# Six full dummy products at the top, and block 0's second half decoded in round 4 ahead of the Prelu

## The chip, the cores and the metric

The kernel runs on one core of a Trainium2 chip. The metric is the device time of one launch in microseconds (us), the median of three runs. Five things run side by side on the core: TensorE (PE, with its weight loads shown apart as PEld), VectorE (DVE), ScalarE (ACT), GpSimd (POOL), and DMA transfers that SyncE (SP) issues.

## The reference

A chunked linear-attention scan over 4 batches, 8 heads and 768 steps (32 channels and 16 states a head) is followed by a two-layer network on its 3072 tokens of width 256. Cut to what matters:

```
for each chunk c:
    M       = (C_c B_c^T) * L_c                      # L: decays inside the chunk, causal
    y_c     = M x_c + (C_c state) * decay_to_i
    state   = decay_full * state + B_c^T (x_c * decay_from_j)
h   = y @ w_in          # [3072, 256] @ [256, 2048]
g   = max(0.01 * h, h)
out = g @ w_out         # [3072, 2048] @ [2048, 256]
```

The weights come as 64-bit floats and are turned into 32-bit floats on the chip.

## The kernel before, in words

The steps are worked on in 12 chunks of 64. The hidden width is cut in 16 blocks `f` of 128, the tokens in 6 tiles `t` of 512. The order of the work on each engine is the order in which the program is written; each engine works its own list in that order, and an instruction that has to wait holds up all that stand behind it on its engine.

**Start.** While the first inputs arrive, PE runs dummy products of zeros on the tile `idle` (128x512, `keep_warm`, line 276) and then 38 tiny ones of 32x32 (line 303). `sum_rows` (line 380), the first product of use, stands behind them. It needs the logarithms of `la`.

**Rounds.** The loop at line 683 runs rounds `c` = 2 to 12. A round makes, in PE's order: `scores` of chunk c (line 465), the first layer of block `f = c - 3` for tile 0 (`ffn_in`, line 192), `outputs` of chunk c-1 (lines 553 and 565), `states` (line 483), a decay product for chunk c+2 (`decays`, line 522), the second layer of the block before (`ffn_out`, line 161), and the other decay product. DVE multiplies the scores with the decays (`weigh`, line 473), decodes weights, makes the low part `gl` of the hidden values (line 199) and keeps the states (`keep_state`, line 495). ACT makes exponentials, the copies `cm` of C (`spread_c`, line 456), the two Prelus of `ffn_in` (lines 196 and 197), and copies of the outputs (line 575).

**Decoding a weight block.** A block's 64-bit words land in `raw` (line 101), 256 KB in a half. `dec_abs` (ACT, line 112), `dec_clamp`, `dec_shift`, `dec_sign`, `dec_low` (DVE, lines 116, 122, 129, 136) turn them into 32-bit floats in `w32`. `dec_high` (ACT, line 142) copies these into the high part `wha`, and `dec_rest` (line 145, POOL or DVE) writes what is left into the low part `wla`. Each product of the network is made three times, high by high, low by high, high by low. Block 0's columns for the first layer (IN) and for the second (OUT) are decoded apart. `ffn_out` of block 0, at the end of round 4, is the first to need the OUT half.

**After the scan** the remaining blocks are decoded in a loop over (f, t) steps up to some 150 us, and tiles 2 to 5 are worked on by a seven-product scheme for 2x2 matrices, in which PE is nearly never idle.

Of the kernel before, what the change touches and what calls it, by code (L numbers as in the profile page):

```python
# [36 lines left out]
DIRECT = 2  # L37
STACKED = (3, 4)
SLOTS = 5
WARM = 3  # L40
SHORT = 38
AHEAD = 4
FIRST = 3
NEARLY = NC - FIRST + 1
# [8 lines left out]
def scan_ffn(ctx: ExitStack, tc: tile.TileContext, a_l, bcn_l, x_l, w_l, out_l):  # L53
    nc = tc.nc
    PSUM = bass.MemoryType.PSUM
    dve, act, pool, pe, sp = nc.vector, nc.scalar, nc.gpsimd, nc.tensor, nc.sync
# [31 lines left out]
    def weight(half, f):  # L88
        return wa[half][:, f] if f < NFA else wb[half][:, f - NFA]
# [13 lines left out]
    def w32(f):  # L103
        if f not in w32s:
            w32s[f // 2 * 2] = w32_pool.tile([128, 2, 2 * DM], F32, name="w32")
            w32s[f // 2 * 2 + 1] = w32s[f // 2 * 2]
        return w32s[f][:, f % 2]

    ALL, IN, OUT = slice(None), slice(0, DM), slice(DM, 2 * DM)

    def dec_abs(f, c=ALL):
        act.activation(w32(f)[:, c], raws[f][:, c, 1].bitcast(F32), AF.Abs)

    def dec_clamp(f, c=ALL):
        w = w32(f)[:, c]
        dve.tensor_scalar(
            out=w, in0=w, scalar1=MAG_MIN, scalar2=MAG_MAX, op0=ALU.max, op1=ALU.min,
        )

    def dec_shift(f, c=ALL):  # L120
        w = w32(f)[:, c].bitcast(U32)
        dve.tensor_scalar(
            out=w, in0=w, scalar1=3, scalar2=0x3FFFFFFF,
            op0=ALU.logical_shift_left, op1=ALU.bitwise_and,
        )

    def dec_sign(f, c=ALL):
        w = w32(f)[:, c].bitcast(U32)
        dve.scalar_tensor_tensor(  # L129
            out=w, in0=raws[f][:, c, 1], scalar=0xC0000000, in1=w,  # L130
            op0=ALU.bitwise_and, op1=ALU.bitwise_or,
        )

    def dec_low(f, c=ALL):
        w = w32(f)[:, c].bitcast(U32)
        dve.scalar_tensor_tensor(
            out=w, in0=raws[f][:, c, 0], scalar=29, in1=w,
            op0=ALU.logical_shift_right, op1=ALU.bitwise_or,
        )

    def dec_high(f, c=ALL):
        act.copy(weight(0, f)[:, c], w32(f)[:, c])  # L142

    def dec_rest(f, eng=None, c=ALL):
        (eng or dve).tensor_tensor(  # L145
            out=weight(1, f)[:, c], in0=w32(f)[:, c], in1=weight(0, f)[:, c], op=ALU.subtract
        )
# [56 lines left out]
    pa, pb = (psum.tile([128, 2, TS], F32, name=n) for n in ("pa", "pb"))  # L204
# [24 lines left out]
    idle = cst.tile([128, TS], BF16, name="idle")  # L229
# [44 lines left out]
    def keep_warm(n, space):  # L274
        for _ in range(n):
            pe.matmul(
                space, lhsT=idle[:, :128], rhs=idle[:, :space.shape[-1]], start=True, stop=True
            )
# [20 lines left out]
        dve.memset(blk[64 * hp:64 * hp + 64, hp], 1.0)  # L299
    dve.memset(later, 0.0)  # L300
    keep_warm(WARM, pa[:, 0])
    for _ in range(SHORT):
        pe.matmul(pa[:32, 0, :32], lhsT=idle[:, :32], rhs=idle[:, :32], start=True, stop=True)
    pool.affine_select(
        out=sign, in_=sign, pattern=[[-3, 2 + GB]], compare_op=ALU.is_ge, fill=0.0, base=-ROW,
        channel_multiplier=1,
# [151 lines left out]
    def scores(c):  # L458
        for b in range(NB):
            bp, st = divmod(b, 2)  # L460
            o = (st * NH2 + bp) * Q
            cols = slice(o, o + Q)
            for g in range(NG):
                r = slice(32 * g, 32 * g + 32)
                pe.matmul(  # L465
                    sspace[g // 2][64 * st:64 * st + 64, g % 2, bp].rearrange(
                        "p (h i) -> p h i", h=2),
                    lhsT=bs[c][r, cols], rhs=cms[c][r, :, cols], start=True, stop=True,
                )

    def weigh(c, half):
        m = lts[c].rearrange("p (a g h) i -> p a g (h i)", a=NH2, g=NG)[:, :, 2 * half:2 * half + 2]
        dve.tensor_tensor(
            out=m, in0=sspace[half].rearrange("p g a x -> p a g x"), in1=m, op=ALU.mult,
        )

    def states(c):
        for b in range(NB):
            bp, st = divmod(b, 2)
            r = slice(64 * st, 64 * st + 64)  # L480
            for g in range(NG):
                u = (bp * NG + g) * 2
                pe.matmul(  # L483
                    zspace(c)[32 * g:32 * g + 32, st * NH2 + bp],
                    lhsT=bnd[c][r, u:u + 2].rearrange("p h n -> p (h n)"),
                    rhs=xs[c][r, u:u + 2].rearrange("p h d -> p (h d)"),
                    start=True, stop=True, skip_group_check=True,
                )
# [38 lines left out]
    def passed(c):  # L527
        for st in range(2):
            pe.matmul(
                espace[:, st * NH2:(st + 1) * NH2], lhsT=esel,  # L530
                rhs=er[:, (c - STACKED[0]) * 2:(c - STACKED[0]) * 2 + 2, st * Q:(st + 1) * Q],
                start=True, stop=True, skip_group_check=True,
            )

    def passed_exp(c):
        es[c] = p3.tile([128, CT], F32, name="es")
        act.activation(
            by_part(es[c]), espace.rearrange("p (s b) i -> p s b i", s=2), AF.Exp
        )
# [45 lines left out]
    def split_out(o, low):  # L585
        hi, lo, v = (v[:, :, o * CT:(o + 1) * CT] for v in (xh[1], xl[1], xf1))
        if low:
            pool.tensor_tensor(out=lo, in0=v, in1=hi, op=ALU.subtract)
        else:
            pool.tensor_copy(hi, v)  # L590
# [85 lines left out]
    def next_decay(c, h):  # L676
        if c < NC:
            if h == 0:
                alloc_lt(c)
            decays(c, h)  # L680
            decay_exp(c, h)

    for c in range(2, NC + 1):
        f = c - FIRST
        if c < NC:
            scores(c)
        if c < AHEAD:
            states(c - 1)
        if c + 1 in STACKED:
            passed(c + 1)  # L690
            passed_exp(c + 1)
        if c == 2:
            for h in range(2):
                next_decay(3, h)
            dec_abs(0, IN)
        if c < NC:
            weigh(c, 1)
            weigh(c, 0)
        if c < AHEAD:
            keep_state(c - 1)  # L700
        if c == 3:
            dec_abs(1)
        if c + 1 < NC:
            spread_c(c + 1)
            weigh_c(c + 1)
        if c < NC - 1:
            weigh_b(c)
        if 6 <= c < 10:
            split_out(*divmod(c - 6, 2))
        if f >= 0:  # L710
            low = ffn_in(f, 0, HB[0])
        else:
            fill_slots(3, 4, dve.tensor_copy)
            dec_clamp(0, IN)
            dec_shift(0, IN)
            send_rows(5, 7)
            send_cols(5, NC, sp)
            fetch_bc(4, "t")
            fetch_w(2, (0,))
            fetch_exp(5)  # L720
            fetch_bc(5, "bc")
            fetch_w(2, (1,))

        if c == 4:
            dec_high(0, OUT)
            dec_rest(0, pool, OUT)
        if c > 2:
            for g in (dec_clamp, dec_shift, dec_sign, dec_low):
                g(f + 1)
        if c > 3:  # L730
            fetch_bc(c + 2, "b")
        if c > 2:
            fetch_w(c, (0,))
        if c > 3:
            fetch_bc(c + 2, "c")
        outputs(c - 1)
        if AHEAD <= c < NC:
            states(c - 1)
        keep_out(c - 1)
        if f >= 0:  # L740
            low()
        if c == 3:
            dec_abs(0, OUT)
            for g in (dec_clamp, dec_shift, dec_sign, dec_low):
                g(0, OUT)
        if AHEAD <= c < NC:
            keep_state(c - 1)
        if c == 2:
            end_decay(c)
            low_out(1)  # L750
        if c > 2:
            fetch_w(c, (1,))
        if c > 3:
            fetch_exp(c + 2)
        if c > 2:
            fetch_bc(c + 2, "t")
            fetch_x(c + 1)
        if c in (4, 7):
            send_rows(*{4: (7, 10), 7: (10, 12)}[c])
        next_decay(c + 2, 0)  # L760
        if c > 2:
            decode_high(f + 1)
            if c < NC - 1:
                end_decay(c)
            if f + 2 <= NFA:
                dec_abs(f + 2)
        if len(queue) > 1:
            ffn_out(*queue.popleft())
        else:
            keep_warm(2, HB[0] if c == 2 else o01[:, 1])  # L770
        if c == 2:
            decays(4, 1)
            dec_sign(0, IN)
            dec_low(0, IN)
            dec_high(0, IN)
            dec_rest(0, pool, IN)
            decay_exp(4, 1)
        else:
            next_decay(c + 2, 1)
# [247 lines left out]
```

## Time and profile before

| | |
|---|---|
| median of 3 runs | 324.14 us (318.23, 324.14, 324.59) |
| profiled execution | 323.78 us |
| its span on the core | 322.1 us |
| PE busy | 307.0 us (95%), 3049 instructions |
| PE weight loads | 238.8 us, 3049 instructions |
| DVE / ACT / POOL busy | 216.9 / 188.1 / 83.4 us |

The sum below is made against the profiled execution. A row of the timeline gives start, duration, engine, line and operation, and in brackets how long the engine had been idle before it and what ended that. The chain of waits follows the work that ended last back to its start; its rows give start, length, engine and line.

### The profile page before, as it was taken

How to read it: one execution, taken by the hardware profiler on the slowest of the kernel's cores; microseconds unless marked ns; L12 is line 12 of the kernel's file. 1: busy time of each engine (PE TensorE's matmuls, PEld its weight loads, DVE VectorE, ACT ScalarE, POOL GpSimd, SP SyncE). 2: the span in 40 equal slices, each digit the busy share in tenths (PEclk: the TensorE clock that was granted, in tenths of full speed). 3: DMA queues.
4: the chain of work that ended last, by engine and by line, in shares of the span. 5: the costliest groups of instructions: out<-in, count | busy, mean ns of one | idle time of the engine just before them, and what ended most of it. 6: DMA issues, size and time to landing. Idle time of an engine off the chain costs nothing.

```text
span 322.1 us, 7449 instructions
## 1 busy us (share of the span) xinstructions
PE 307.0 (95%) x3049; PEld 238.8 (74%) x3049; DVE 216.9 (67%) x354; ACT 188.1 (58%) x353; POOL 83.4 (26%) x115
## 2 busy tenths in 40 slices
PE   8987799997999999999999999999999999999994
PEld 4444477665688887887878888888888888888883
DVE  6589478886789498853776566676576555665551
ACT  7675767774375567654764467644576436554451
POOL 6245347564267345951000100000000000000000
PEclk9999899998999999999999999999999999999999
DMA  6576976664124000000020000000003000000003
GB/s 184 145 239 169 293 247 188 201 186 160 58 78 133 1 0 0 2 0 0 26 107 0 0 1 3 0 0 2 0 18 113 2 0 0 2 1 0 1 2 130
DMA packets 17926, 21.67 MB, mean 67 GB/s; under 512 B 3300, under 2 KB 10724, under 8 KB 17892
## 3 DMA queue, kind: packets, MB, share of 16 engines
q1 hardware_dynamic: 17732, 21.16, 21.1%
q8 instruction: 24, 0.39, 0.5%
q14 instruction: 10, 0.08, 0.1%
q10 hardware_dynamic: 160, 0.04, 0.1%
HBM read 17.80 MB, written 3.39 MB: 66 GB/s over the span
## 4 chain that ended last, share of the span: by engine, by line
PE 78%; DVE 8%; ACT 5%; issue 4%; POOL 1%; DMA 1%; SPq 0%; DVEq 0%; ACTq 0%; POOLq 0%
PE o L161 35%; PE h L161 22%; PE h L192 8%; PE pa L465 2%; PE pa L553 1%; DVE w L129 1%; DMA raw<-w_l 1%; PE pa L565 1%; DVE wlb L145 1%; ACT h L197 1%; DVE gl L199 1%; PE pd L522 1%; PE pb L483 1%; PE pb L565 1%; ACT gh L196 1%
## 5 line engine op out<-in xcount | busy, mean ns | idle before, releaser
L935 ACT ACTIVATE gh<-tmp 128x512 fp32r<-128x512 f32 x48 | 30.2, 629 | 49.7 <-DVE tmp L959 46.4
L161 PE MATMUL o<-gh,wha 128*128 128x512 f32 x132 | 53.2, 403 | 1.2 <-ACT wha L142 1.2
L161 PE MATMUL o<-gl,wha 128*128 128x512 f32 x132 | 52.2, 396 | 0.5 <-DVE gl L199 0.5
L161 PE MATMUL o<-gh,wla 128*128 128x512 f32 x132 | 52.2, 396 | 0.3 <-POOL wla L145 0.3
L937 DVE TENSOR_TENSOR gl<-tmp,gh 128x512 fp32r<-128x512 f32 x48 | 33.2, 692 | 22.2 <-ACT tmp L936 22.2
L199 DVE TENSOR_TENSOR gl<-h,gh 128x512 fp32r<-128x512 f32 x32 | 21.8, 684 | 14.4 <-ACT h L197 14.4
L196 ACT ACTIVATE gh<-h 128x512 fp32r<-128x512 f32 x32 | 19.1, 597 | 21.1 <-PE h L192 21.1
L936 ACT ACTIVATE tmp<-tmp 128x512 f32<-128x512 f32 x48 | 30.3, 632 | 1.5
L161 PEld LDWEIGHTS o<-gh,wha 128*128 128x128 f32 x132 | 25.0, 189 | 6.6 <-ACT wha L142 1.5
L161 PEld LDWEIGHTS o<-gl,wha 128*128 128x128 f32 x132 | 25.2, 191 | 6.3 <-DVE gl L199 1.0
L161 PEld LDWEIGHTS o<-gh,wla 128*128 128x128 f32 x132 | 24.9, 189 | 5.7 <-POOL wla L145 0.6
L161 PE MATMUL h<-oph,wsh 128*128 128x512 f32 x64 | 25.0, 391 | 0.0
L161 PE MATMUL h<-oph,wsl 128*128 128x512 f32 x64 | 24.9, 389 | 0.0
L161 PE MATMUL h<-opl,wsh 128*128 128x512 f32 x64 | 24.9, 389 | 0.0
L954 DVE TENSOR_TENSOR tmp<-h,tmp 128x512 f32<-128x512 f32 x16 | 11.1, 691 | 19.9 <-PE h L161 19.9
L145 POOL TENSOR_TENSOR wla<-w,wha 128x512 fp32r<-128x512 f32 (+1 forms) x12 | 14.3, 1193 | 35.3 <-ACT wha L142 32.8
L161 PE MATMUL o<-gh,whb 128*128 128x512 f32 x60 | 23.3, 389 | 0.0
L161 PE MATMUL o<-gh,wlb 128*128 128x512 f32 x60 | 23.3, 389 | 0.0
L161 PE MATMUL o<-gl,whb 128*128 128x512 f32 x60 | 23.3, 389 | 0.0
L952 ACT COPY tmp<-h 128x512 f32<-128x512 f32 x16 | 9.4, 590 | 20.8 <-PE h L161 20.8
L197 ACT ACTIVATE h<-h 128x512 f32<-128x512 f32 x32 | 19.0, 595 | 0.0
L192 PE MATMUL h<-xh,wha 128*128 128x512 f32 x44 | 18.5, 420 | 0.0
(176 smaller groups left out, 695.7 us busy)
## 6 DMA issues: line engine op xcount, KB each, us to landing
raw<-w_l SPq DMA_DIRECT2D x32, 256.0 KB
xs<-x_l SPq DMA_DIRECT2D x12, 256.0 KB
out_l<-ob SPq DMA_DIRECT2D x9, 256.0 KB
bs<-bcn_l SPq DMA_DIRECT2D x12, 128.0 KB
cs<-bcn_l SPq DMA_DIRECT2D x12, 128.0 KB
ts<-bcn_l SPq DMA_DIRECT2D x12, 128.0 KB
es<-esums SPq DMA_DIRECT2D x18, 64.0 KB
out_l<-wtmp SPq DMA_DIRECT2D x3, 256.0 KB
```

Source lines behind the costliest of these rows:

```text
L145: (eng or dve).tensor_tensor(out=weight(1, f)[:, c], in0=w32(f)[:, c], in1=weight(0, f)[:, c], op=ALU.subtract)
L161: pe.matmul(space, lhsT=w, rhs=x, start=start and i == 0, stop=stop and i == 2, skip_group_check=again,)
L192: pe.matmul(hp, lhsT=w[k][low_w], rhs=(xh, xl)[low_x][t][:, k], start=i == 0, stop=i == 5,)
L196: act.activation(gh, hp, AF.Prelu, alpha=0.01)
L197: act.activation(hp, hp, AF.Prelu, alpha=0.01)
L199: return lambda: dve.tensor_tensor(out=gl, in0=hp, in1=gh, op=ALU.subtract)
L465: pe.matmul(sspace[g // 2][64 * st:64 * st + 64, g % 2, bp].rearrange("p (h i) -> p h i", h=2), lhsT=bs[c][r, cols], rhs=cms[c][r, :, cols ...
L935: act.activation(gh, v, AF.Prelu, alpha=0.01)
L936: act.activation(v, v, AF.Prelu, alpha=0.01)
L937: return g, lambda: dve.tensor_tensor(out=gl, in0=v, in1=gh, op=ALU.subtract)
L952: act.copy(a, A)
L954: dve.tensor_tensor(out=u2, in0=B, in1=a, op=ALU.add)
```

## The change

`WARM` goes from 3 to 6 and the 38 tiny products are gone. In round 3, `dec_sign` and `dec_low` of block 0's OUT half no longer stand at the end of the round. They stand in round 4 behind the two `weigh` of that round, with `dec_high` and `dec_rest` of that half right behind them, ahead of `ffn_in`; and `dec_rest` is on DVE where it was on POOL.

```
-WARM = 3
-SHORT = 38
+WARM = 6
...
     keep_warm(WARM, pa[:, 0])
-    for _ in range(SHORT):
-        pe.matmul(pa[:32, 0, :32], lhsT=idle[:, :32], rhs=idle[:, :32], start=True, stop=True)
...
         if 6 <= c < 10:
             split_out(*divmod(c - 6, 2))
+        if c == 4:
+            dec_sign(0, OUT)
+            dec_low(0, OUT)
+            dec_high(0, OUT)
+            dec_rest(0, dve, OUT)
         if f >= 0:
             low = ffn_in(f, 0, HB[0])
...
-        if c == 4:
-            dec_high(0, OUT)
-            dec_rest(0, pool, OUT)
         if c > 2:
             for g in (dec_clamp, dec_shift, dec_sign, dec_low):
                 g(f + 1)
...
         if c == 3:
             dec_abs(0, OUT)
-            for g in (dec_clamp, dec_shift, dec_sign, dec_low):
-                g(0, OUT)
+            dec_clamp(0, OUT)
+            dec_shift(0, OUT)
```

DVE from the end of round 3 to the end of round 4, before (`w32_461` with 256 columns is block 0's OUT half, `w32_689` block 2, `lt_547` the decays of chunk 4, `ss_807` the states that chunk 4's outputs read):

```order
L199 TENSOR_TENSOR gl0_61<-h0_89,gh0_60 128x512
L116 TENSOR_SCALAR w32_461<-w32_461 128x256
L122 TENSOR_SCALAR w32_461<-w32_461 128x256
L129 SCALAR_TENSOR_TENSOR w32_461<-raw_393,w32_461 128x256
L136 SCALAR_TENSOR_TENSOR w32_461<-raw_393,w32_461 128x256
L473 TENSOR_TENSOR lt_547<-pb_95,lt_547 128x2x256
L473 TENSOR_TENSOR lt_547<-pa_94,lt_547 128x2x256
L116 TENSOR_SCALAR w32_689<-w32_689 128x512
L122 TENSOR_SCALAR w32_689<-w32_689 128x512
L129 SCALAR_TENSOR_TENSOR w32_689<-raw_483,w32_689 128x512
L136 SCALAR_TENSOR_TENSOR w32_689<-raw_483,w32_689 128x512
L199 TENSOR_TENSOR gl1_63<-h0_89,gh1_62 128x512
```

The same stretch of DVE in the changed kernel, whose line numbers are one lower at the top and three lower from line 304 on (`w32_426` is block 0, `w32_652` block 2, `lt_512` chunk 4's decays):

```order
L115 TENSOR_SCALAR w32_426<-w32_426 128x256
L121 TENSOR_SCALAR w32_426<-w32_426 128x256
L470 TENSOR_TENSOR lt_512<-pb_95,lt_512 128x2x256
L470 TENSOR_TENSOR lt_512<-pa_94,lt_512 128x2x256
L128 SCALAR_TENSOR_TENSOR w32_426<-raw_358,w32_426 128x256
L135 SCALAR_TENSOR_TENSOR w32_426<-raw_358,w32_426 128x256
L144 TENSOR_TENSOR wla_59<-w32_426,wha_58 128x256
L115 TENSOR_SCALAR w32_652<-w32_652 128x512
L121 TENSOR_SCALAR w32_652<-w32_652 128x512
L128 SCALAR_TENSOR_TENSOR w32_652<-raw_448,w32_652 128x512
L135 SCALAR_TENSOR_TENSOR w32_652<-raw_448,w32_652 128x512
L198 TENSOR_TENSOR gl1_63<-h0_89,gh1_62 128x512
```

The two multiplications come two instructions earlier; the sign, the low bits and the new `wla` stand between them and block 2's decoding.

ACT in round 4, before (`raw_483` is block 2, `lt_682` chunk 5's decays, `gh1` and `h0` the Prelus of block 1):

```order
L112 ACTIVATE w32_689<-raw_483 128x512
L449 ACTIVATE lt_682<-pd_96 128x512
L456 ACTIVATE cm_713<-cs_490,odd_131 128x256 x2
L196 ACTIVATE gh1_62<-h0_89 128x512
L197 ACTIVATE h0_89<-h0_89 128x512
L142 CAST wha_58<-w32_461 128x256
L575 COPY xf1_126<-pa_94 128x256
```

and in the changed kernel:

```order
L111 ACTIVATE w32_652<-raw_448 128x512
L446 ACTIVATE lt_645<-pd_96 128x512
L453 ACTIVATE cm_676<-cs_455,odd_131 128x256 x2
L141 CAST wha_58<-w32_426 128x256
L195 ACTIVATE gh1_62<-h0_89 128x512
L196 ACTIVATE h0_89<-h0_89 128x512
L572 COPY xf1_126<-pa_94 128x256
```

The copy of block 0's OUT half has passed the two Prelus; it still stands behind block 2's `dec_abs`.

## Rows read from the trace of the kernel before

**Rows 1.** The page, its fourth part: the chain's shares of the span by engine.
```profile
PE 78%; DVE 8%; ACT 5%; issue 4%; POOL 1%; DMA 1%; SPq 0%; DVEq 0%; ACTq 0%; POOLq 0%
```

**Rows 2.** The chain of waits in order of time: start us, us, what.
```profile
1.26 1.46 PE pa L276 x3
2.72 1.12 PE pa L303 x38
...
28.98 3.88 DMA raw<-w_l
...
34.03 0.80 ACT cm L456 x2
...
36.19 0.74 POOL wla L145
36.98 1.91 PE o L161 x5
...
39.33 0.41 PE pa L465 x2
40.42 1.93 PE h L192 x6
...
98.63 0.60 DVE wlb L145
```

**Rows 3.** Timeline of PE, 1 to 14 us.
```profile
6.92 1.91 PE L373 MATMUL pd<-lt,after 128*128 128x512 f32 x2
...
11.73 1.12 PE L373 MATMUL pd<-lt,after 128*128 128x512 f32 x2
```

**Rows 4.** Timeline of ACT, round 4.
```profile
35.72 0.39 ACT L142 CAST wha<-w 128x256 fp32r<-128x256 f32 x1
```

**Rows 5.** Timeline of DVE, end of round 3 and round 4.
```profile
29.42 1.38 DVE L129 SCALAR_TENSOR_TENSOR w<-raw,w 128x256 uint32<-128x256 uint32 x1
...
33.58 0.43 DVE L116 TENSOR_SCALAR w<-w 128x512 f32<-128x512 f32 x1 [0.82 <-ACT w L112]
...
35.23 0.69 DVE L136 SCALAR_TENSOR_TENSOR w<-raw,w 128x512 uint32<-128x512 uint32 x1
...
36.76 0.61 DVE L495 SCALAR_TENSOR_TENSOR ss<-pb,odd,tmp 128x128 f32<-128x128 f32 x2 [0.24 <-ACT xf L575]
```

**Rows 6.** Timeline of POOL at the same time.
```profile
29.19 1.33 POOL L145 TENSOR_TENSOR wla<-w,wha 128x512 fp32r<-128x512 f32 x1 [3.14 <-ACT wha L142]
```

**Rows 7.** The chain of waits at the start of round 10.
```profile
71.64 0.53 DVE ss L495 x2
...
72.21 0.33 PE pb L465 x2
```

**Rows 8.** Stretches: busy us (count) of PE, PEld, DVE, ACT, POOL; granted clock; DMA share; GB/s.
```profile
37.00:42.00 5.00, 5.00 (x44) 3.23 (x44) 1.85 (x5) 2.63 (x6) 3.17 (x4) 0.66 0.85 218
78.00:83.00 5.00, 4.94 (x63) 3.34 (x63) 1.28 (x4) 1.48 (x3) 1.86 (x2) 0.66 0.30 103
```

**Rows 9.** Timeline of PE: the two waits in `states` that no engine ended.
```profile
57.09 0.33 PE L483 MATMUL pb<-xs,bnd 64*32 64x64 f32 x10 [1.04 <-issue]
...
78.06 0.42 PE L483 MATMUL pb<-xs,bnd 64*32 64x64 f32 x21 [2.02 <-issue]
```

**Rows 10.** The page, its third part: queue, kind: packets, MB, share of 16 engines.
```profile
q8 instruction: 24, 0.39, 0.5%
```

**Rows 11.** The same view of 54.4 to 55.6 us alone.
```profile
q8 instruction: 1, 0.02, 5.2%
```

**Rows 12.** Stretches, columns as in rows 8: counts of PE's instructions between places.
```profile
57.05:78.05 21.00, 18.52 (x511) 13.29 (x512) 17.15 (x29) 14.44 (x30) 12.12 (x14) 1.00 0.59 179
52.43:55.83 3.40, 3.40 (x152) 2.62 (x134) 2.87 (x5) 2.40 (x6) 3.40 (x5) 1.00 0.82 271
39.79:43.73 3.94, 3.94 (x147) 2.95 (x136) 3.10 (x6) 2.30 (x6) 1.31 (x2) 0.83 0.83 235
59.47:62.86 3.39, 3.39 (x144) 2.60 (x137) 2.72 (x5) 2.55 (x6) 3.39 (x5) 1.00 0.55 186
```

## The prediction, made before the changed kernel had run

> **What bounds the kernel now.** I read the chain of waits first. PE holds 78% of it, and "issue", time in which PE waited for nothing that the profile shows, holds 4% [rows 1]. Behind some 150 us PE is never let down, and the change touches nothing there, so all that it can win or lose lies in the first 90 us. In the chain in order of time I looked for the pieces that are not PE's around the edited places [rows 2]: the dummies at the top, and the stretch from 28.98 to 40.42. Third I read the timeline of each engine there: what each instruction waited for, and what stood behind it [rows 4 to 6]. Fourth come the stretches with a granted clock under 1 [rows 8], and last PE's waits for "issue", the longest of which the chain runs through [rows 9].
>
> **The top.** Three dummies take 1.46 us of the chain, the 38 tiny products 1.12 [rows 2]. [...]
>
> **Round 4, the second layer's weights.** Block 2's second half lands at 28.98 + 3.88 = 32.86 [rows 2], and its `dec_abs` heads ACT's list in this round; the edit leaves it there, and no DMA is issued elsewhere in SP's order. ACT is through with exponential and `cm` at 34.83. Before, two Prelus followed, then the copy at 35.72, then POOL's `wla` until 36.93, and PE's products with `wla` began at 36.98 [rows 2, 4]. Now the copy comes at 34.83 and takes 0.39 [rows 4]: 35.22. `dec_rest` on DVE, 256 columns: the nearest row has 512 in 0.60 [rows 2], so 0.3 to 0.4 if it is free; the other bound is 1.38, which 256 columns of `dec_sign` took while a POOL instruction ran from 29.19 to 30.52 [rows 5, 6]. POOL has nothing at 35, so I take 0.4: 35.6. PE's second layer could go on **1.35 us** earlier. The Prelus come 0.39 later, and their readers (`gl` on DVE, the second layer a round later) have more room than that.
>
> What is late next is DVE. It stands in `dec_rest` until the copy has come, and behind that stand block 2's four decoding steps (33.58 to 35.92 before), `gl` and `ss`, which ended at 37.37 [rows 5]. From 33.58 to 37.37 less 0.24 idle is 3.55 us; from 35.6 on it ends at 39.15. `scores` of the next round wait for `ss` (in round 10, 71.64 + 0.53, then 72.21) [rows 7]. Before, they ran from 39.33 to 40.42, delayed by PE itself, which had the lower clock from 37.7 [rows 2, 8]. Now they start at 39.2 or so: 0.1 earlier, not 1.35. If the clock doesn't fall, they and the first layer behind them (1.09 and 1.93 us in those rows) are faster by some 0.7; PE is idle in this stretch in both kernels, so I give that an even chance. POOL's `wla` of block 2 comes about 0.9 later than at 37.74, for its copy waits for `dec_low` on DVE, and is still done before the last two of the six products that need it. Loads into `raw` that wait for block 2's buffer come free at 37.95 and are issued behind that. Term: -0.1 to -0.8, **-0.5 us**.
>
> The other half of the edit, the two `weigh` ahead of sign and low bits, takes 1.38 and 0.73 us out of the way of `outputs`, but what PE does next waits for the half that lands at 32.86, so it hides. Sign and low bits have from 31 to 35 to themselves.
>
> **PE's instruction stream.** 24 packets of 0.39 MB in all on the instruction queue are 16 KB each, for 6098 instructions of PE, 254 to a packet [rows 10]. The waits of 1.04 and 2.02 us stand 511 + 512 instructions apart, which is four times 256 [rows 9, 12]; and in 54.4 to 55.6 one such packet moved, ahead of the release at 57.09 [rows 11]. So I read both as waits for a block of 256 instructions that came late. It is late where 256 instructions are used up quickly: from 52.43 to 55.83 PE went through scores, first layer, outputs and most of states, 3.40 us without the second layer in between [rows 12], while DMA was 82% busy and the packet could come only 2 to 3 us after the block had begun. With 70 fewer instructions (76 out, 6 in) every block ends 70 later. Both places then fall into the next round's start, and these waits go: 1.04 + 2.02 = 3.1 us. Behind the second the clock fell: 5 us at a mean of 0.66 are 5 x 0.34 = 1.7 us lost [rows 8]. Together 4.8.
>
> But other blocks now end in `states`: of rounds 5, 8 and 11. Their 256 instructions took 3.94 us (at a clock of 0.83) and 3.39 before [rows 12]; in round 11 DMA rests (share 0.30 in that part [rows 8]), so the packet comes at once. For the other two, 2.1 us from the block's begin to the packet, 1.0 for it and 1.4 until PE goes on (as at 57.09) are 4.5 us against 3.4: 1.1 to 1.3 each, 2.4 with a little for round 11, an estimate from these rows. I take it that no clock falls for them, as none fell behind the 1.04. Term: -4.8 + 2.4, **-2.4 us**; its ends are -4.8 (no new wait) and 0 (the new ones as dear).
>
> [...]
>
> **Sum.** 323.8 (profiled) + 0.2 - 0.5 - 2.4 = **321.1 us**. The profiled execution lies 0.4 under the median of 324.14; one run of the three had 318.23.
>
> **Rivals.**
> First, the waits stay as dear: the two belong to their place in `states`, not to the stream, or the three new ones with one fall of the clock cost 4.8 again. For it: DMA is as busy in rounds 5 and 8 as it was at the old places. Against it: the distance of exactly four blocks. 323.8 + 0.2 - 0.5 = 323.5. Chance 0.28, from 322.4 to 325. [...]
>
> [...] Chance 0.18, from 315.5 to 319.5.
>
> Third, slower: `dec_rest` on DVE becomes the bound of rounds 4 and 5. If it or the two-input decoding steps behind it meet a POOL instruction, each is held as at 29.42: 1.38 for 0.3 to 0.4, so 1.0 apiece, two of them 2.0. `ss` then ends at 41.1, `scores` start 1.8 later than before, PE stands idle long enough for the clock to fall once more (1.7), and with the waits as dear as before 323.8 + 0.2 + 1.8 + 1.7 = 327.5. It decides from the point where `ss` ends behind 39.3. Against it: POOL waits for ACT's copy of block 2 in this stretch and has nothing to run. Chance 0.10, from 325 to 329.
>
> The forecast has 0.42, 319.5 to 322.4. The edit may also do nothing, because the copy stays behind the late half; that is 0.5 of the sum and lies inside the forecast.
>
> **Numbers.** The likeliest is 321.1. From 316.5 to 325.0 I leave out the third rival, a third of the second and little of the first: 0.82 inside. Two per cent, about what a measurement of this kernel can tell from no change (its runs are 2.0% apart), is 6.5 us: under 317.7 lies some 0.08 from the second rival, over 330.6 0.02, and 0.90 between.
>
> **What would show it.** Right: no wait for "issue" in `states` of rounds 7 and 10, shorter ones in `states` of rounds 5 and 8, the granted clock at 1.00 around 78; PE's first product with block 0's `wla` near 35.6 and DVE's `ss` near 39.1. Wrong: waits at the old places (the stream is not the cause), or `ss` behind 40 (the third rival), or the product of rows 3 at 1.12 us near 7 (the early clock, and a time under 319).

## The result and the profile after

| | before | changed |
|---|---|---|
| median of 20 runs | 321.40 us | 323.25 us |
| profiled execution | 323.78 us | 323.70 us |
| ratio | | 1.0064, 95% interval 1.0036 to 1.0093 |

The ratio, here and below, is that of the fast runs alone (those within 1.5% of a kernel's fastest), so it differs a little from the ratio of the medians of all runs, which is 1.0058 here.

The changed kernel is 0.6% slower; 321.1 us and a small gain had been forecast. The two profiled executions are as long as each other, and that has to be kept in mind in all that follows: the one of before lies 2.4 us over the median of its 20 runs, the changed one 0.45 over its own. A difference of 1.9 us in the medians can't be read off these two traces alone; it takes the experiments below. What the traces do show is which of the steps happened.

**The top.** The chain of waits of the changed kernel:

```profile
1.26 2.74 PE pa L275 x6
4.00 1.05 PE o L377 x4
...
19.23 3.78 issue
...
39.19 0.68 DVE gl L198
39.87 0.53 DVE ss L492 x2
41.13 1.59 PE h L191 x6
```

The six dummies take 2.74 us, where 1.46 + 1.12 stood [rows 2]: 0.16 more. The timeline of PE has `sum_rows` at 3.79, 0.02 later than before, and then the products of [rows 3]:

```profile
3.79 1.26 PE L377 MATMUL o<-upto,la 128*128 128x128 f32 x4
...
6.16 1.02 PE L370 MATMUL pd<-lt,after 128*128 128x512 f32 x2
7.02 1.02 PE L370 MATMUL h<-lt,after 128*128 128x512 f32 x2
```

1.02 us at 6.16, where 1.91 had been needed at 6.92: the products were fast early, and that part of the second rival did come. The prediction and the expectations call it the early clock, but the granted clock of the profile doesn't show it: it is 1.00 from 6.9 to 8.9 us before and 1.00 from 6.1 to 8.1 us here. What makes these products faster isn't shown. Nor is it shown that the six dummies brought it: two executions of kernels with the old top (the low part on POOL, and sign and low bits alone, both below) have the same product as early and as fast:

```profile
5.91 1.02 PE L373 MATMUL pd<-lt,after 128*128 128x512 f32 x2
...
6.08 1.02 PE L373 MATMUL pd<-lt,after 128*128 128x512 f32 x2
```

**PE's stream.** The timeline of PE in the outputs of round 2, in `states` of rounds 5, 8 and 11, and in a later group of outputs:

```profile
18.69 0.54 PE L562 MATMUL pb<-lt,xs 64*32 64x64 f32 x27
23.01 0.43 PE L562 MATMUL pb<-lt,xs 64*32 64x64 f32 x5 [3.78 <-issue]
...
45.26 0.33 PE L480 MATMUL pb<-xs,bnd 64*32 64x64 f32 x11 [0.91 <-issue]
...
64.89 0.42 PE L480 MATMUL pb<-xs,bnd 64*32 64x64 f32 x21 [0.69 <-issue]
...
84.09 0.46 PE L480 MATMUL pb<-xs,bnd 64*32 64x64 f32 x31 [0.33 <-issue]
...
89.50 0.33 PE L562 MATMUL pb<-lt,xs 64*32 64x64 f32 x11 [0.49 <-issue]
```

The waits of 1.04 and 2.02 us [rows 9] are gone; the three foreseen ones are there, with 0.91, 0.69 and 0.33 us. The last one, 0.49 us, was not on the list, and the first line's wait, 3.78 us in the middle of a product group, was not foreseen at all. The stretches around that long wait, and the one around 78 us (columns as in [rows 8]):

```profile
15.80:19.02 3.22, 2.43 (x127) 1.71 (x128) 2.47 (x6) 2.48 (x7) 2.29 (x4) 1.00 0.88 248
...
22.00:30.00 8.00, 6.73 (x95) 3.98 (x99) 4.02 (x10) 3.76 (x9) 2.04 (x3) 0.57 0.63 175
77.00:79.00 2.00, 2.00 (x101) 1.73 (x94) 1.93 (x4) 1.50 (x4) 0.00 (x0) 1.00 0.04 8
```

From 15.8, where PE went on behind a wait of 0.5 us that the profile puts down to POOL, to this one PE used up 127 + 128 instructions, one block, in 3.2 us, while DMA was 88% busy. A packet of 16 KB, by the author's reading the next block's, moved only behind that (the instruction queue in 20.1 to 21.6 us):

```profile
q8 instruction: 1, 0.02, 5.5%
```

The clock fell behind it: 8 us at a mean of 0.57 are 8 x 0.43 = 3.4 us of PE's time at most, an estimate (PE was busy for 6.73 of the 8). Around 78, where 1.7 us had been lost [rows 8], it is 1.00.

**Round 4.** The timeline of ACT (the copy of block 0's OUT half), and that of DVE:

```profile
36.16 0.41 ACT L141 CAST wha<-w 128x256 fp32r<-128x256 f32 x1 [1.31 <-DVE w L135]
...
36.59 0.43 DVE L144 TENSOR_TENSOR wla<-w,wha 128x256 fp32r<-128x256 f32 x1 [0.47 <-ACT wha L141]
...
39.79 0.60 DVE L492 SCALAR_TENSOR_TENSOR ss<-pb,odd,tmp 128x128 f32<-128x128 f32 x2
```

The low part takes 0.43 us on DVE (0.4 was taken), and `ss` comes at 39.79 where it had stood at 36.76 [rows 5]. ACT was free for the copy at 34.85, as forecast, but stood 1.31 us until DVE had made sign and low bits: these came late, behind a round 4 that PE, held up in round 2, had begun late. PE's products with block 0's low part began at 37.43, not near 35.6; they had begun at 36.98 before [rows 2]. PE then stood 1.04 us for `ss` in `scores` of round 5:

```profile
40.45 0.33 PE L462 MATMUL pb<-cm,bs 32*64 32x128 f32 x2 [1.04 <-DVE ss L492]
```

### The profile page after: what moved, and what is told of

Same layout as the page of the kernel before. It is cut to its first block, busy times and chain, and to the rows that moved or that the text cites. A ratio compares the mean times of both kernels' runs of the same rounds, so it can differ in the third digit from the quotient of the medians.

```text
span 322.0 us, 7377 instructions
## 1 busy us (share of the span) xinstructions
PE 304.7 (95%) x3012; PEld 237.9 (74%) x3014; DVE 216.8 (67%) x355; ACT 188.3 (58%) x353; POOL 82.9 (26%) x114
## 4 chain that ended last, share of the span: by engine, by line
PE 73%; DVE 13%; issue 6%; ACT 3%; DMA 2%; POOL 1%; SPq 0%; DVEq 0%; ACTq 0%; POOLq 0%
PE o L160 33%; PE h L160 22%; PE h L191 7%; DVE w L128 3%; DVE gl L198 2%; DVE lt L470 1%; PE pa L462 1%; DMA bs<-bcn_l 1%; PE pb L462 1%; DVE wlb L144 1%; PE pa L550 1%; PE pa L275 1%; DVE w L115 1%; DMA raw<-w_l 1%; PE pb L562 1%
## 5 line engine op out<-in xcount | busy, mean ns | idle before, releaser
L160 PE MATMUL o<-gl,wha 128*128 128x512 f32 x132 | 51.5, 390 | 0.6 <-DVE gl L198 0.6
L160 PE MATMUL o<-gh,wla 128*128 128x512 f32 x132 | 51.4, 389 | 0.0
L144 POOL TENSOR_TENSOR wla<-w,wha 128x512 fp32r<-128x512 f32 (+1 forms) x11 | 13.5, 1228 | 36.8 <-ACT wha L141 32.9
```

Source lines behind the costliest of these rows:

```text
L144: (eng or dve).tensor_tensor(out=weight(1, f)[:, c], in0=w32(f)[:, c], in1=weight(0, f)[:, c], op=ALU.subtract)
L160: pe.matmul(space, lhsT=w, rhs=x, start=start and i == 0, stop=stop and i == 2, skip_group_check=again,)
```

## The experiments

Theory S: the loss is PE's stream of instructions. 70 fewer put a block's end where PE uses up its instructions fast (255 in 3.2 us) and DMA is busy (88%). By this theory a wait of PE that no engine ended is a wait for the next block's packet, and is called so below. Theory D, the rival: the loss is the decoding, DVE being late in round 4. Every ratio is to before in runs on the same chip, with its 95% interval. The first four kernels ran on one chip, the next four on a second, the last four on a third; where two ratios from different chips are set against each other, each is against before on its own.

**The top alone.** Six dummies, no tiny products, the decoding as before:

```
-WARM = 3
-SHORT = 38          # and the loop of tiny products
+WARM = 6
```

> The top alone: six full dummies, no tiny products, the decoding as before. Theory S (the stream of PE's instructions): the 70 instructions fewer put a block's end into the outputs of round 2, where PE waited 3.8 us in the changed kernel; this kernel has the same wait of 3 to 4 us after 19 us and a time like the changed one's, 1.004 to 1.010 of before. Theory D (the decoding: DVE late in round 4) has the loss in round 4 alone: this kernel is at 0.995 to 1.000 of before, since the early clock stays as a gain.

Measured: 1.0106 (1.0054 to 1.0157), 322.34 against 320.52 us. The wait is there, in the same place (timeline of PE):

```profile
20.92 0.31 PE L562 MATMUL pb<-lt,xs 64*32 64x64 f32 x5 [2.42 <-issue]
```

It is 2.42 us long, under the 3 to 4 expected, and the time lies just above the range that theory S gave. The top alone is slower, although PE begins the outputs of round 2 at 17.07 us in it and at 20.01 before.

**The decoding alone.**

```
+        if c == 4:
+            dec_sign(0, OUT); dec_low(0, OUT); dec_high(0, OUT); dec_rest(0, dve, OUT)
```

> The moved decoding alone, the top as before. Theory S: no block's end moves, so no wait in round 2; PE's waits for nothing the profile shows stay in states of rounds 7 and 10; time 0.997 to 1.002 of before. Theory D: the states of round 4 end late on DVE (after 39 us), scores of round 5 wait for them, and the time is 1.004 to 1.010 of before.

Measured: 1.0040 (1.0004 to 1.0076), 321.10 us. So there is something in theory D as well. Of the waits of PE's weight loads between 34 and 41 us (engine, line, waited for: us, times, longest):

```profile
PEld o L161 <- ACT wha L142: 1.5, 1, 1.5
PEld pb L465 <- DVE ss L495: 1.3, 1, 1.3
```

and DVE's timeline:

```profile
39.10 0.60 DVE L495 SCALAR_TENSOR_TENSOR ss<-pb,odd,tmp 128x128 f32<-128x128 f32 x2
```

`ss` at 39.1 to 39.7, and `scores` of round 5 stand 1.3 us for it; 0.4% of 320 us is 1.3 us, though the interval reaches from 0.1 to 2.4 us, and by the medians of all runs it is 1.0018. PE's waits for packets stayed at their old places in rounds 7 and 10.

**The shorter stream alone**, with the old dummies:

```
-SHORT = 38
+SHORT = 3
```

> Before with 3 tiny products in place of 38: PE's stream is 70 instructions shorter, as in the changed kernel, with no denser dummies and the old decoding. Theory S, if the block's end alone decides: a wait of 2 to 4 us in the outputs of round 2, waits in states of rounds 5 and 8 and none in rounds 7 and 10, time 1.003 to 1.010 of before. If it takes the early clock as well (PE ahead of its packets), the wait in round 2 is under 1 us and the time is 0.990 to 1.000. Theory D: 0.997 to 1.002, waits where they were.

Measured: 1.0216 (1.0172 to 1.0260), 326.22 us, over twice the loss expected at most: the largest loss of all comes from leaving out 35 products that compute nothing.

```profile
20.89 0.54 PE L565 MATMUL pb<-lt,xs 64*32 64x64 f32 x27
26.02 0.43 PE L565 MATMUL pb<-lt,xs 64*32 64x64 f32 x5 [4.58 <-issue]
```

The wait of 4.58 us comes after the same 27 products. An earlier start of these outputs isn't needed for it: PE begins the outputs of round 2 at 20.01 us before and at 20.00 here. The other waits lay in `states` of rounds 5, 8 and 11, as in the changed kernel. Why is the loss twice that of the top alone? The first products of the outputs of round 2 and the wait in `states` of round 8, in the kernel with the top alone and in this one:

```profile
17.07 0.27 PE L550 MATMUL pa<-cd,ss 32*64 32x64 f32 x2 [0.75 <-DVE lt L470]
63.14 0.42 PE L480 MATMUL pb<-xs,bnd 64*32 64x64 f32 x21 [0.95 <-issue]
...
20.00 0.27 PE L553 MATMUL pa<-cd,ss 32*64 32x64 f32 x2 [0.75 <-POOL cd L544]
68.07 0.42 PE L483 MATMUL pb<-xs,bnd 64*32 64x64 f32 x21 [0.38 <-issue]
```

Behind the wait of round 2 this kernel is 5.1 us later (26.02 against 20.92): 2.9 from the later start of these outputs (20.00 against 17.07), 2.2 from the longer wait. In round 8 it still is 4.9 us later.

**The changed kernel with the stream filled up again**: 37 tiny products for the two full dummies behind the masks.

```
-    keep_warm(2, pa[:, 0])
+    for _ in range(37):
+        pe.matmul(pa[:32, 0, :32], lhsT=idle[:, :32], rhs=idle[:, :32], start=True, stop=True)
```

> The changed kernel with 37 tiny products in place of the two full dummies behind the masks: from there on PE's stream counts as before, while the six full dummies stay. Theory S: block ends lie where they lay before; waits return to states of rounds 7 and 10, the wait in round 2 shrinks to 2 us or less, and the time is 0.992 to 1.001 of before. Theory D: like the changed kernel, 1.004 to 1.010.

Measured: 1.0044 (1.0006 to 1.0083), 321.05 us. PE had no wait for a packet in round 2 any more, and one of 0.62 us in `states` of round 10, so the trace is as theory S has it. The time isn't: it lies in the range of theory D, and only 0.2% under the changed kernel's 1.0064, less than either interval can tell. What is left is about as much as the decoding alone cost (1.0040); that it is this loss is argued from the size.

**The low part on POOL**, with the decoding moved and the top as before:

```
-            dec_rest(0, dve, OUT)
+            dec_rest(0, pool, OUT)
```

> The moved decoding with the low part on POOL as before, the top as before; beside the run with the moved decoding alone (1.004 of before). Theory D1: the loss of the moved decoding is that VectorE stands in the low part until ScalarE's copy has come, with block 2's decoding and the states behind it. Then the states of round 4 end near 37.4 us and not at 39.7, scores of round 5 wait for them no longer (1.3 us there), and the time is 0.996 to 1.001. Theory D2: the loss is the Prelus coming 0.4 us later, or sign and low bits standing behind the multiplications: time as with the moved decoding alone, 1.002 to 1.007.

Measured: 0.9978 (0.9946 to 1.0009), 319.82 us, against 1.0040 with DVE. DVE's timeline:

```profile
36.09 0.59 DVE L495 SCALAR_TENSOR_TENSOR ss<-pb,odd,tmp 128x128 f32<-128x128 f32 x2
```

`ss` is 3.0 us earlier, and no wait of `scores` for it is among PE's waits. Not all of the 3.0 is the low part's new place, for block 2's weights came earlier here. Their `dec_abs` with the decoding alone, and in this kernel:

```profile
33.61 0.69 ACT L112 ACTIVATE w<-raw 128x512 f32<-128x512 f32 x1 [4.13 <-DMA raw<-w_l]
...
31.97 0.66 ACT L112 ACTIVATE w<-raw 128x512 f32<-128x512 f32 x1 [4.62 <-DMA raw<-w_l]
```

Counted from there `ss` comes 5.49 us later with the low part on DVE and 4.12 on POOL, against 3.88 before: the low part on DVE costs `ss` 1.4 us. This is theory D1: the copy's new place and the order of sign and low bits cost next to nothing; an instruction on DVE that waits for ACT does, with block 2's four decoding steps, whose input is there, in line behind it.

**Sign and low bits alone** behind the multiplications:

```
-            for g in (dec_clamp, dec_shift, dec_sign, dec_low): g(0, OUT)
+            dec_clamp(0, OUT); dec_shift(0, OUT)      # sign and low in round 4
```

> Of the moved decoding only sign and low bits behind the multiplications of round 4; copy and low part where they were and on POOL. Theory D1: no loss, 0.997 to 1.001, the outputs of chunk 3 start about 1 us earlier and nothing follows from it. Theory D2 (the order of sign and low bits costs): 1.002 to 1.007.

Measured: 0.9990 (0.9957 to 1.0023), 321.10 us. It neither costs nor gives, as D1 has it.

**A longer stream**, before with 35 tiny products for the two dummies behind the masks (66 instructions more).

> Before with 35 tiny products in place of the two dummies behind the masks: PE's stream is 66 instructions longer. Theory S (blocks of 256 instructions): every block ends 66 instructions earlier in the program; the block ends that lie late in a burst are then in rounds 4 and 9. No wait in states of rounds 7 and 10, one of 0.5 to 1.5 us in states of round 9, none over 1 us in the outputs of round 2; time 0.993 to 1.003. If place and not count decides, the waits stay in rounds 7 and 10.

Measured: 0.9962 (0.9927 to 0.9996), 319.94 us. The waits for packets in PE's timeline (round 3, round 9):

```profile
24.91 0.34 PE L483 MATMUL o<-xs,bnd 64*32 64x64 f32 x14 [1.37 <-issue]
...
69.36 0.32 PE L483 MATMUL pb<-xs,bnd 64*32 64x64 f32 x8 [0.68 <-issue]
```

One more of 0.6 us lay at the end of round 6. In rounds 7 and 10 PE is never idle where the two waits had been (55 to 57 and 74 to 77 us, PE busy 2.00 of 2 and 3.00 of 3):

```profile
55.00:57.00 2.00, 2.00 (x108) 1.77 (x101) 1.93 (x3) 1.74 (x5) 0.78 (x1) 1.00 0.86 222
74.00:77.00 3.00, 3.00 (x134) 2.38 (x126) 2.90 (x6) 2.41 (x6) 0.53 (x2) 1.00 0.23 85
```

So the count decides, not the place. The wait in round 9 was foreseen, that in round 4 didn't show, and round 3's was not on the list. All traces together say the same. When PE's products and weight loads are numbered in order, with the few semaphore and drain instructions among them, all 38 waits of PE over 0.3 us that no engine ended, in the fourteen kernels of this document, stand at a number that leaves 191 to 195 when it is divided by 256 (194 and 193 before; 193, 191, 192, 191 and 192 in the changed kernel).

**Loads issued later**, in the kernel with the shorter stream: block 1's two halves (512 KB) behind the columns of the decays.

```
-    fetch_w(1)
...
             send_cols(5, NC, sp)
+            fetch_w(1)
```

> The kernel with the stream 70 shorter and the old decoding (1.022 of before, a wait of 4.7 us in the outputs of round 2), with the two loads of block 1's weights (512 KB) issued later, behind the columns of the decays in round 2. Theory S with the packet late because DMA is busy: the packet that stands behind these loads comes 1.5 to 3 us earlier, the wait shrinks from 4.7 to 2 or less, and the time goes from 1.022 to 1.005 to 1.015 (block 1 may then come late itself). If the packet's time has nothing to do with the loads, the wait stays at 4 to 5 us.

Measured: 1.0111 (1.0084 to 1.0137), against 1.0216 with the loads in their place.

```profile
24.89 0.43 PE L565 MATMUL pb<-lt,xs 64*32 64x64 f32 x5 [2.83 <-issue]
```

The wait went from 4.58 to 2.83 us, not under 2 as expected, and the time by 1%. This fits a packet that is late in part because of these loads. The wait alone couldn't show it: with the loads in their place it was 2.42, 3.78 and 4.58 us in three kernels, one execution each. What keeps the packet for the rest isn't shown.

**Four combinations.** The low part on POOL and the longer stream together:

> The moved decoding with the low part on POOL (0.998 of before) and PE's stream 66 instructions longer (0.996 of before) together. Theory S with D1: the two are apart in the program and add up, 0.990 to 0.997; waits of PE in rounds 3, 6 and 9, none in states of rounds 7 and 10; states of round 4 done before 37 us. If the gain of either was chance of its runs: 0.997 to 1.003.

Measured: 0.9988 (0.9957 to 1.0020), 320.54 us. The gains of the two didn't add up; either may have been some 0.2% less than its runs showed. PE waited for packets in rounds 3 and 9 (1.73 and 0.70 us), as expected, and not in round 6; `ss` of round 4 came at 38.17, not before 37.

The six full dummies with the old decoding and 37 tiny products for the two dummies behind the masks:

> The six full dummies with the decoding as before, and 37 tiny products in place of the two dummies behind the masks, so that PE's blocks end where they did before. What is left of the change is the denser start alone. Theory S: the loss of the top alone (1.011) was the shifted stream: now 0.995 to 1.002, no wait over 2 us in round 2. If the denser start itself costs, 1.005 to 1.012. If the early clock is worth what the rows say (1.6 us and more), 0.990 to 0.996; if loads hold round 3 anyway, 0.997 to 1.002.

Measured: 1.0034 (1.0003 to 1.0064), 320.96 us, in none of the four ranges. With the shifted stream mended no wait for a packet is left in round 2, and most of the loss of the top alone (1.0106) is gone, but the denser start gives nothing. PE's timeline of this kernel shows where an early lead ends:

```profile
7.11 1.02 PE L370 MATMUL h<-lt,after 128*128 128x512 f32 x2
...
28.34 0.61 PE L519 MATMUL pd<-dr,dl 118*128 118x512 bf16 x1 [3.37 <-DMA dl<-sums]
```

It took 1.02 us for this product at 7.11 already, and its exponential `erev` came at 8.66 instead of 11.06. At 28.34 PE had waited 3.37 us for the columns of the decays (`dl`), which SP issues behind the big loads; before, the same product ran at 27.11. The lead of 2.4 us is gone in this wait. The kernel with sign and low bits alone, early with the old top, loses its lead in the same place: it waits 2.49 us for `dl` and runs that product at 27.12.

The moved decoding on POOL and 14 tiny products for the two dummies (24 instructions more):

> The moved decoding with the low part on POOL and 14 tiny products in place of the two dummies behind the masks: PE's stream 24 instructions longer. Theory S: blocks end 24 instructions earlier than before, still within the bursts of rounds 7 and 10 but in the outputs and not in states; waits there shrink by the time of 24 instructions, some 0.2 to 0.3 us each, time 0.992 to 0.999.

Measured: 0.9965 (0.9935 to 0.9994), 319.26 us, with the longer stream above the fastest of all kernels here. Its one long wait for a packet, 0.79 us, still lay in `states` of round 7, 12 products earlier than before, and not in the outputs as expected; that of round 10 was gone.

The changed kernel with both repairs:

> The changed kernel with both repairs: blocks of PE's stream as before (37 tiny products for the two dummies) and the low part on POOL. Theory S with D1: nothing is left of the loss, 0.993 to 0.999 of before, 0.005 to 0.01 below the same kernel with the low part on VectorE (1.004). If the loss had another cause, 1.002 to 1.006.

Measured: 0.9989 (0.9955 to 1.0023), against 1.0044 for the same with the low part on DVE and 1.0064 for the changed kernel. By the ratio nothing of the loss is left. By the medians of all runs the two stand alike, at 1.0015 and 1.0017 (320.77 against 320.30, 321.05 against 320.52 us), so the size of this gain is open. Its mechanism shows in the traces: counted from block 2's `dec_abs`, `ss` comes 4.11 us later here (38.94 behind 34.83) and 5.45 with the low part on DVE (39.52 behind 34.07).

## Why the prediction was wrong, point by point

**The stream was read rightly, its list was not complete.** That 256 instructions make a block (the 38 waits at 191 to 195 of 256), that both old waits would go and that blocks would newly end in `states` of rounds 5, 8 and 11 all came true; the three waits together (1.9 us) were under the 2.4 taken. (The stretches of [rows 12] that gave it hold 281 to 286 instructions and not 256, so the blocks went faster than was read there; the size came out well all the same.) The step that failed is the sentence "other blocks now end in `states`: of rounds 5, 8 and 11". It looked at full rounds alone. In round 2, which has no first layer, another block now ended after 27 of 32 products of the outputs, at the time when DMA was 88% busy, and PE waited 3.78 us for it, with up to 3.4 us of lower clock (0.57 from 22 to 30 us) behind. The term of -2.4 should have been a loss: with the shorter stream alone the runs have +2.2%, 7 us, with the top alone +1.1%, with the stream filled up again +0.3%.

**The base of the sum was an unlucky execution.** The profiled one of before held both waits and a fall of the clock behind the second, and the term of -4.8 took their whole price off. The median of 20 runs, 321.40, lies 2.4 us under it. The six other kernels above whose blocks end where they did before show what is rare. Five of them have waits of 2.0 to 2.9 us at the two places together, and one has 0.6. But the clock from 76 to 84 us is 1.00 in five of the six; only with sign and low bits alone did it fall there (0.79, as before). So the 1.7 us for the clock is a price that few executions pay, and a clock of 1.00 around 78 was no sign of the change.

**That 323.25 lies inside 316.5 to 325.0, and close to the first rival's 323.5, is luck.** The range stood on a base 2.4 us too high. The first rival, in one of its two forms, had new waits and a fall of the clock as dear as the old, but in `states`, and not the one wait in round 2 that the runs show.

**Round 4 had nearly the right time and the wrong comparison.** `ss` was to end at 39.15; it ended at 39.7 with the decoding alone, and at 40.4 in the changed kernel, where sign and low bits did not "have from 31 to 35 to themselves": they ended at 36.1. The term of -0.5 set `ss` against `scores` at 39.33, which in that execution had been held up by the low clock (0.66 from 37 to 42 us [rows 8]). With only sign and low bits moved `ss` came at 36.41 and `scores` began at 38.21, without a wait; that is the measure, and the term is a loss of some 1.3 us (0.1 to 2.4 by the runs). The third rival had this mechanism (DVE's wait in the low part) and asked for a POOL instruction in the way; none was needed. Its sign, `ss` behind 40, came too. That it decides "from the point where `ss` ends behind 39.3" was close.

**The products at the top were fast early, and on the stream as it was that gave nothing.** The second rival (chance 0.18, from 315.5 to 319.5) had no new wait, no fall of the clock at 37.7 and these products early. It took 1.6 us for the last, two pairs at 1.91 - 1.12 [rows 3], and put it down to the clock; no run shows that cause, with 1.00 granted before and after. PE did take 1.02 us for the product at 6.2, but the first rows of a lead are not its end. With the dense start and the stream filled up again a DMA wait in round 3 (3.37 us) took it back. On the shifted stream it was worth something, some 2.9 us between the top alone and the shorter stream alone, but the wait in round 2 cost more. The sign "the early clock, and a time under 319" so came true by half, as far as the product's time goes. No run shows the term of +0.2 for the dummies: the six of them took 0.16 us more than the three and the tiny products, and `sum_rows` began 0.02 later.

**At its block ends this kernel does wait.** Waits of 0.3 to 4.6 us are shown above at them, and one count of instructions or another makes 2% of the time (1.0216 with 70 fewer, 0.9962 with 66 more).

**What stays open.** Top alone and decoding alone would make 1.0146 together; both at once measured 1.0064 (1.0036 to 1.0093). The intervals reach each other, just. It may be that the long wait in round 2 lets loads catch up, so that round 4 costs less behind it; no run tells that apart. How the 0.6% divides between stream and decoding in the changed kernel is therefore not shown: each was shown to cost by itself (the decoding barely clear of no change), and both waits are in its trace, but the changed kernel with the low part on POOL and its stream left short was not run. Nor was it settled why the dense start with the stream mended is still at 1.0034; with both repairs the same start is at 0.9989, so it may be chance.

## What to carry to other kernels

A dummy or a tiny product is also an instruction: in this kernel, 70 instructions fewer moved the waits behind them (1.04 and 2.02 us in `states` of rounds 7 and 10 went, 3.78 us in the outputs of round 2 came), and two waits "for nothing" 511 + 512 instructions apart [rows 12] were the sign to look for. When an instruction is moved onto another engine, put it behind what doesn't have to wait for its input, or on an engine that is idle then (POOL here, 0.9978 against 1.0040 on DVE). And take a long wait, and above all a fall of the clock behind it, off a sum only when several executions show it: the fall around 78 was in two of seven here (before, and with sign and low bits alone).

## What was not expected of the hardware

Leaving out 35 products that compute nothing made the kernel 2.2% slower (1.0216). In the changed kernel PE stood 3.78 us in the outputs of round 2, behind a stretch in which DMA was 88% busy, and a packet of 16 KB on the instruction queue moved within that wait (20.1 to 21.6 us); in the kernel with the shorter stream PE stood 4.58 us, and 2.83 when 512 KB of loads were issued later.
